# First x tiles loaded one by one between the value rows, in natural token order, and turned by whole 128x128 transposes

## The chip, the cores and the metric

The kernel runs on one core of a Trainium2 chip. The core has five engines with queues of their own, which work at the same time and wait for one another by semaphores: TensorE (PE in the profile, its weight loads PEld), VectorE (DVE), ScalarE (ACT), GpSimd (POOL) and SyncE (SP), which here issues most of the transfers (DMAs). Matmul results land in PSUM, eight banks of 512 float32 columns in 128 partitions; everything else lies in SBUF.

The metric is the device time of one execution in microseconds (us). Before the change it is 283.16 us, the median of three runs (283.02 to 283.38).

## What is computed

A gated mix of two branches over the same x, 2048 tokens of 640 values in bf16: linear attention with 32 heads of 20, and a GELU-gated feed-forward of width 1728.

```python
def _A_ref(x, wqkv, w_phi, wo):
    qkv = (x @ wqkv).reshape(B, S, 3, H, Dh).transpose(2, 0, 3, 1, 4)
    q, k, v = qkv[0], qkv[1], qkv[2]
    pq = einsum("bhsd,hdf->bhsf", q, w_phi)
    pk = einsum("bhsd,hdf->bhsf", k, w_phi)
    phi_q = concatenate([softmax(pq), softmax(-pq)], -1)
    phi_k = concatenate([softmax(pk), softmax(-pk)], -1)
    kv = einsum("bhsf,bhsd->bhfd", phi_k, v)
    z  = einsum("bhsf->bhf", phi_k)
    num = einsum("bhqf,bhfd->bhqd", phi_q, kv)
    den = einsum("bhqf,bhf->bhq", phi_q, z)[..., None] + 1e-6
    return (num / den).transpose(0, 2, 1, 3).reshape(B, S, D) @ wo

def _B_ref(x, w_gate, w_up, w_down):
    return (gelu(x @ w_gate) * (x @ w_up)) @ w_down

g = sigmoid((x * gate_w).sum(-1, keepdims=True))
return g * _A_ref(x, ...) + (1 - g) * _B_ref(x, ...)
```

## The kernel before

**Tiling.** Tokens go in 16 tiles of 128 (`t` = 0 to 15), the 640 model columns in five slices of 128 (`kt`). `xT` holds x turned, 640 rows in five slices by 2048 tokens, because a matmul contracts over the partitions. `w3` holds the value columns of wqkv, one gate column and the folded key and query weights side by side.

**Order.** It is written out by hand: each engine runs its instructions in the order of the program, and a small class (`_Sched`) puts in the semaphore waits from what each operation reads and writes. A PE instruction that waits holds all behind it; so does a waiting copy on DVE or ACT.

**The start.** SP issues, in this order (lines 247 to 262): two loads of the first 512 tokens into `xtok`; the value columns of wqkv, row slice by row slice, the first slice in two pieces (columns 0 to 255 and the rest); a part of w_up (`wue`); the turning transfers of x tiles 4 and 5, of the key weights (`wkT`), of x tiles 6 and 7; another part of w_up (`wul`); the turning transfers of the query weights (`wqT`) and of x tiles 8 to 15. Tiles 0 to 3 are turned on PE instead. In them the tokens are taken with a stride: partition p of tile j holds token 4p + j, so that one load of two tiles reads 2,560 contiguous bytes for a partition, and the output rows of these tiles are written back in the same order (line 919).

ACT issues two small loads, w_phi (line 276, behind the second of POOL's masks) and the gate vector `gz` (line 279).

PE begins in `attention_state` (line 670) with matmuls on constants that nothing reads (line 675). Then come the transposes of tiles 0 and 1 (line 342, 64x64 blocks, ten a tile), six more matmuls on constants (line 682), tiles 2 and 3; each tile goes to PSUM and is copied to `xT` by DVE, by ACT, or by both. Then the value products of tiles 0 to 3 (`v_step`, line 478): for each `kt` and tile a matmul of 480 and one of 160 columns, those of `kt` = 0 cut at column 256. Before the last round `blockdiag` (DVE, line 361) spreads w_phi into block-diagonal tiles, and `gate_column` (line 367) turns the gate vector into a column of `w3`. The finished values are copied out (`v_first_evac`).

**Behind it.** `up_ahead` (line 546) computes three blocks of the feed-forward early, from `wue` and x tiles 0 to 3; then the value tiles 4 and 5, the fold of w_phi into the key weights (`fold`, line 404, reads `wkT` and the block-diagonal tiles), value tiles 6 and 7, key tile 0, two more early blocks from `wul`, the fold into the query weights, and so on through all tiles. The feed-forward and the output follow. The gate's logit of a token tile comes out of one added column, either in the value product or, where `k_gate` (line 560) says so, in the key product.

Of the kernel before, what the change touches and what calls it, by code (L numbers as in the profile page):

```python
# [3 lines left out]
P = 128  # L4
BF16 = mybir.dt.bfloat16
F32 = mybir.dt.float32
AF = mybir.ActivationFunctionType
# [100 lines left out]
class _Kernel:  # L108
    S, D, H, DH, F = 2048, 640, 32, 20, 1728
# [112 lines left out]
    def loads(self):  # L222
# [4 lines left out]
        x4 = self.x[0:self.BT, :].rearrange("(p j) n -> p j n", j=self.TB)  # L227

        def xload(q, j):
            sc.dma(q, lambda e: e.dma_start(self.xtok[:, j:j + 2, :], x4[:, j:j + 2, :]),  # L230
                   writes=[("xtok", j), ("xtok", j + 1)])
# [33 lines left out]
        for i in range(KD):  # L265
# [67 lines left out]
    def x_transpose(self, t, ek):  # L333

        sc = self.sc
        b, w = (0, 4, 2, 6)[t], self.D // 2
        bks = (b, b + 1)
        pv = self.bank(b, 1024).bitcast(BF16).rearrange("p (r c) -> p r c", r=2)[:, :, 0:w]
        for c in range(self.KD):
            for r in (0, 1):  # L340
                a = 64 * r
                sc.op("pe", lambda e: e.transpose(
                    pv[:, r, c * 64:(c + 1) * 64], self.xtok[a:a + 64, t, c * P:(c + 1) * P],
                    self.ident[a:a + 64, a:a + 64]),
                    reads=[("xtok", t), "ident"], writes=[("ps", bks[r])], signal=(c == self.KD - 1))
        out = self.xT[:, :, t * P:(t + 1) * P].rearrange("p c (r t) -> p c r t", t=64)
        src = pv.rearrange("p r (c t) -> p c r t", t=64)
        rd = [("ps", b) for b in bks]
        if ek == "ad":
            sc.op("act", lambda e: e.activation(out[:, :, 0, :], src[:, :, 0, :], AF.Copy), reads=rd[:1], writes=[("xh", t)])  # L350
            sc.op("dve", lambda e: e.tensor_copy(out[:, :, 1, :], src[:, :, 1, :]), reads=rd[1:], writes=[("xT", t)])
        elif ek == "a":
            sc.op("act", lambda e: e.activation(out, src, AF.Copy), reads=rd, writes=[("xT", t)])
        else:
            sc.op("dve", lambda e: e.tensor_copy(out, src), reads=rd, writes=[("xT", t)])
# [117 lines left out]
    def v_step(self, t, kt, part=None):  # L473
        sc = self.sc
        tail = (480, 160, 4 + t // 3, 160 * (t % 3))
        parts = ([(0, self.VA, t, 0)], [(self.VA, 480 - self.VA, t, self.VA), tail], [(0, 480, t, 0), tail])
        for c0, n, bk, col in parts[2 if part is None else part]:
            sc.op("pe", lambda e, c0=c0, n=n, bk=bk, col=col: e.matmul(  # L478
                self.bank(bk)[:, col:col + n], self.xT[:, kt, t * P:(t + 1) * P], self.w3[:, kt, c0:c0 + n],
                start=(kt == 0 and col == 0), stop=(kt == self.KD - 1), skip_group_check=True),  # L480
                reads=[("xT", t), ("xh", t), "wv0" if part == 1 else ("wv", kt)], writes=[("ps", bk)],
                signal=(kt == self.KD - 1))
# [18 lines left out]
    def v_part(self, t, b, part):  # L501
# [4 lines left out]
        self.proj(t, n, self.D + 1 - n, b + 1, 0, ["wv", "wgate"])  # L506
# [4 lines left out]
        self.gate_exp(t, b + 1, o + self.D)  # L511
# [48 lines left out]
    def k_gate(self, t):  # L560
        return 1 if t < self.TB or t == 5 else 0
# [108 lines left out]
    def attention_state(self):  # L670
# [3 lines left out]
        for n in (512, 512, 512, 512, 512, 512, 128, 128, 128):  # L674
# [3 lines left out]
        xt(0, "d")  # L678
        xt(1, "a")
        for i in range(3):  # L680
            for a, b in ((0, 2), (64, 3)):
                sc.op("pe", lambda e: e.matmul(self.bank(b, P), ones[a:a + 64, 0:P], ones[a:a + 64, 0:P], start=True,
                                               stop=True), writes=[("ps", b)])
# [14 lines left out]
        ve([3], "d", True)  # L698
        v, k, q = self.v_tile, self.k_tile, self.q_tile
# [3 lines left out]
        v(4, 2)  # L703
        self.v_split(5, 0)
# [172 lines left out]
    def down_pair(self, t0, banks, widths):  # L877
# [25 lines left out]
        def evac(h):  # L903
# [14 lines left out]
            if t0 < self.TB:  # L918
# [120 lines left out]
```

## Time and profile before

| what | value |
|---|---|
| median of the runs | 283.16 us (283.02 to 283.38) |
| span of the profiled execution | 282.4 us |
| PE busy | 278.6 us, 2926 matmuls |
| DVE busy | 173.2 us |
| ACT busy | 105.9 us |
| POOL busy | 15.1 us |
| granted TensorE clock | 1.000 |
| read from device memory | 9.04 MB |
| written to it | 2.62 MB |

The span runs from the first to the last instruction on the device; the time of a run is a little longer. Times in the timeline count from the span's start. A row of it is a start, a duration, the engine and line, the operation, and what it writes from what it reads; "xN" says that N such instructions in a row are merged. A matmul's duration includes its way through the array, so the spacing of successive starts, not the duration, tells what one costs PE. Transfers are told by the size of each and the time from issue to landing.

The slices of the busy row show where PE is not fully busy: the first of 40 slices (7 us each) has 7 tenths, the last 6 tenths, all others 9 or more.

```profile
PE   7999999999999999999999999999999999999996
...
PEclk9999999999999999999999999999999999999999
DMA  7999169787789910011000000000133132532221
```

### The profile page before, as it was taken

Reading aid. Unit: us, or ns where it says so; the run is one execution under the profiler, and the core shown is the slowest. Engines: PE = TensorE matmul, PEld = TensorE weight load, DVE = VectorE, ACT = ScalarE, POOL = GpSimd, SP = SyncE. Lnnn points to the kernel's source line nnn. Section 1 sums busy time; section 2 is a strip of 40 time slices with the busy share of each in tenths; the row PEclk is TensorE's granted clock in tenths of the full one; section 3 lists DMA queues with packets and bytes.
Section 4 is the critical chain, followed back from the end, with each engine's and each line's share of the span. In section 5 each row is a group of like instructions: output and inputs, shape, how many; then the busy total and the mean of one; then the engine's idle time right before and its main releaser. Section 6 shows DMA issues by size and latency. Waiting matters only on the chain.

```text
span 282.4 us, 6904 instructions
## 1 busy us (share of the span) xinstructions
PE 278.6 (99%) x2926; PEld 168.6 (60%) x2926; DVE 173.2 (61%) x329; ACT 105.9 (38%) x204; POOL 15.1 (5%) x69
## 2 busy tenths in 40 slices
PE   7999999999999999999999999999999999999996
PEld 4566766665665444444444444445777777777786
DVE  1456999999997523694333324235883883883801
ACT  3246978777793332223232232321112112112011
POOL 7511001101000000000000000000000000000000
PEclk9999999999999999999999999999999999999999
DMA  7999169787789910011000000000133132532221
GB/s 213 193 223 190 29 127 172 153 175 149 157 175 274 350 51 0 2 24 23 2 0 0 0 2 0 0 0 2 26 50 98 46 49 78 66 49 73 73 72 49
DMA packets 60378, 24.11 MB, mean 85 GB/s; under 512 B 51002, under 2 KB 59834, under 8 KB 60346
## 3 DMA queue, kind: packets, MB, share of 16 engines
q1 hardware_dynamic: 59680, 23.63, 38.9%
q8 instruction: 23, 0.38, 0.6%
q10 hardware_dynamic: 666, 0.03, 0.2%
q14 instruction: 9, 0.07, 0.1%
HBM read 9.04 MB, written 2.62 MB: 41 GB/s over the span
## 4 chain that ended last, share of the span: by engine, by line
PE 97%; DMA 1%; SPq 0%; ACT 0%; issue 0%
PE ps L464 58%; PE ps L898 29%; PE ps L599 4%; PE ps L817 2%; PE ps L478 2%; PE ps L637 2%; DMA w<-in_A_wqkv_dram 1%; PE ps L404 1%; SPq L230 0%; SPq L251 0%; ACT outsb L911 0%; PE ps L370 0%
## 5 line engine op out<-in xcount | busy, mean ns | idle before, releaser
L464 PE MATMUL ps<-xT,wu_sb 128*128 128x512 bf16 x260 | 64.1, 379 | 0.0
L464 PE MATMUL ps<-xT,wg_sb 128*128 128x512 bf16 x260 | 63.9, 379 | 0.0
L779 ACT ACTIVATE gl<-ps 128x512 bf16<-128x512 f32 x52 | 31.0, 597 | 70.3 <-PE ps L464 70.3
L464 PE MATMUL ps<-w,xT 128*128 128x362 bf16 (+5 forms) x340 | 51.4, 302 | 0.0
L898 PE MATMUL ps<-wd_sb,hT 64*128 64x320 bf16 x648 | 48.4, 296 | 0.0
L781 DVE TENSOR_TENSOR hT<-ps,gl 128x512 bf16<-128x512 f32 x34 | 23.4, 689 | 37.7 <-PE ps L464 37.7
L464 PEld LDWEIGHTS ps<-xT,wu_sb 128*128 128x128 bf16 x260 | 25.4, 98 | 30.3 <-DVE hT L781 0.2
L464 PEld LDWEIGHTS ps<-xT,wg_sb 128*128 128x128 bf16 x260 | 25.1, 98 | 29.8 <-issue 0.2
L911 ACT ACTIVATE outsb<-ps,Gm 128x320 bf16<-128x320 f32 (+2 forms) x31 | 14.5, 515 | 71.8 <-PE ps L898 71.8
L464 PEld LDWEIGHTS ps<-w,xT 128*128 128x128 bf16 x340 | 31.9, 97 | 14.8
L898 PEld LDWEIGHTS ps<-wd_sb,hT 64*128 64x128 bf16 x648 | 30.9, 94 | 12.2 <-issue 0.4
L898 PE MATMUL ps<-wo_sb,goT 64*128 64x320 bf16 (+2 forms) x340 | 26.5, 288 | 0.0
L617 DVE TENSOR_REDUCE Dk<-Ek 128x66 f32<-128x1320 bf16 x16 | 24.3, 1520 | 2.3 <-ACT gcol L528 2.3
L626 DVE TENSOR_TENSOR Ek<-Ek,Dk 128x1320 bf16<-128x1320 bf16 x16 | 24.5, 1532 | 0.5
L863 DVE TENSOR_TENSOR O<-ps,RH 128x640 bf16<-128x640 f32 x32 | 24.7, 815 | 0.0
L538 ACT ACTIVATE Ek<-ps 128x627 bf16<-128x627 f32 x32 | 20.5, 693 | 6.4 <-PE ps L599 4.9
L538 ACT ACTIVATE Eqt<-ps 128x627 bf16<-128x627 f32 x32 | 20.6, 705 | 2.5 <-PE ps L464 2.5
L781 DVE TENSOR_TENSOR xT<-ps,gl 128x512 bf16<-128x512 f32 x13 | 9.0, 690 | 18.2 <-PE ps L464 18.2
L898 PEld LDWEIGHTS ps<-wo_sb,goT 64*128 64x128 bf16 x340 | 15.9, 94 | 5.3
L898 PE MATMUL ps<-wd_sb,xT 64*128 64x320 bf16 (+2 forms) x270 | 16.0, 269 | 0.0
L851 DVE RECIPROCAL RH<-ps 128x32 f32<-128x32 f32 x16 | 5.7, 357 | 14.4 <-PE ps L817 14.3
L898 PEld LDWEIGHTS ps<-wd_sb,xT 64*128 64x128 bf16 x270 | 12.1, 94 | 2.7
(90 smaller groups left out, 184.1 us busy)
## 6 DMA issues: line engine op xcount, KB each, us to landing
out_dram<-outsb SPq DMA_DIRECT2D x7, 320.0 KB, 2.3
wd_sb<-in_B_w_down_dram SPq DMA_DIRECT2D x1, 2080.0 KB, 11.0
wg_sb<-in_B_w_gate_dram SPq DMA_DIRECT2D x5, 224.0 KB, 3.1
wg_sb<-in_B_w_gate_dram SPq DMA_DIRECT2D x5, 192.0 KB, 3.5
wu_sb<-in_B_w_up_dram SPq DMA_DIRECT2D x5, 192.0 KB, 3.9
wo_sb<-in_A_wo_dram SPq DMA_DIRECT2D x1, 800.0 KB, 9.7
xtok<-in_A_x_dram SPq DMA_DIRECT2D x2, 320.0 KB, 3.3
w<-in_A_wqkv_dram SPq DMA_DIRECT2D x4, 160.0 KB, 4.0
```

Source lines behind the costliest of these rows:

```text
L464: self.sc.op("pe", lambda e: e.matmul(self.ps[:, bank * 512 + c0:bank * 512 + c0 + n], lhs, rhs, start=first, stop=fin), reads=reads, writ ...
L478: sc.op("pe", lambda e, c0=c0, n=n, bk=bk, col=col: e.matmul(self.bank(bk)[:, col:col + n], self.xT[:, kt, t * P:(t + 1) * P], self.w3[:, ...
L538: self.sc.op("act", lambda e: e.activation(dst, src, AF.Exp, scale=scale), reads=[("ps", b), ("ps", b + 1)], writes=[(name, sl, s)])
L599: self.sc.op("pe", lambda e: e.matmul(out, self.xT[:, kt, t * P:(t + 1) * P], self.w3[:, kt, c:c + 2 * n].rearrange("p (r w) -> p r w", w= ...
L617: self.sc.op("dve", lambda e: e.tensor_reduce(self.Dk[:, se, 0, :].rearrange("p (u h) -> p u h", h=self.HG), self.k_view(se), AX.X, ALU.ad ...
L626: sc.op("dve", lambda e: e.tensor_tensor(v, v, R.rearrange("p (u h) -> p u h", h=self.HG).unsqueeze(3).to_broadcast([P, 2 * self.G, self.H ...
L779: sc.op("act", lambda e: e.activation(self.gl[:, slot, :], self.bank(banks[0]), AF.Gelu_apprx_tanh), reads=[("ps", banks[0])], writes=[("g ...
L781: sc.op("dve", lambda e: e.tensor_tensor(hT, up, self.gl[:, slot, :], ALU.mult), reads=[upk, ("gl", slot)], writes=[("hT", hk, c)], guard=old)
L851: dve(lambda e: e.reciprocal(R(0), Dn[1]), rb, [key(0)], guard=old)
L863: dve(lambda e, o=o, f=f, s=s: e.tensor_tensor(o, V[s][:, :, 0:DH], f, ALU.mult), rb + [key(6 + s)], [("O", s, sl)], guard=old)
L898: sc.op("pe", lambda e: e.matmul(self.bank(bk, w), lhs, rhs, start=opens and x == 0, stop=end and not opens, skip_group_check=True), reads ...
L911: sc.op("act", lambda e: e.activation(dst, self.bank(bk, w), AF.Copy, scale=g), reads=rd, writes=wr)
```

## The change

- x tiles 0 to 3 are loaded in natural token order, one load for each tile (160 KB), and these loads alternate with the value row slices: x0, w0, x1, w1, x2, w2, x3, w3, w4. The first value slice comes in one piece.
- A tile is turned by five whole 128x128 transposes. The first three slices go to one PSUM bank and are copied by DVE (key `xh`), the last two to the next bank and are copied by ACT (key `xT`). Value steps with `kt` < 3 wait for the first copy only.
- PE starts with four matmuls of 512 columns and four of 128 on constants instead of six and three; the six small ones behind the first tile have 128 rows instead of 64. The value steps are interleaved with the transposes of the next tiles.
- The loads of w_phi and of the gate vector are issued from ACT behind the last x copy. `blockdiag` moves behind the copies of the first values.
- `gate_column` moves behind value tile 4. The gate logit of tile 4 moves from its value product to its key product.
- The output rows of tiles 0 to 3 are written in natural order.

```diff
-        x4 = self.x[0:self.BT, :].rearrange("(p j) n -> p j n", j=self.TB)
+        x4 = self.x[0:self.BT, :].rearrange("(j p) n -> p j n", p=P)
 
         def xload(q, j):
-            sc.dma(q, lambda e: e.dma_start(self.xtok[:, j:j + 2, :], x4[:, j:j + 2, :]),
-                   writes=[("xtok", j), ("xtok", j + 1)])
+            sc.dma(q, lambda e: e.dma_start(self.xtok[:, j, :], x4[:, j, :]), writes=[("xtok", j)])
...
-        xload("sp", 0)
-        xload("sp", 2)
         for kt in range(KD):
-            for a, z, key in ((0, self.VA, ("wv", 0)), (self.VA, D, "wv0")) if kt == 0 else ((0, D, ("wv", kt)),):
-                sc.dma("sp", lambda e: e.dma_start(self.w3[:, kt, a:z], w3[:, kt, 2 * D + a:2 * D + z]), writes=[key])
+            if kt < self.TB:
+                xload("sp", kt)
+            sc.dma("sp", lambda e: e.dma_start(self.w3[:, kt, 0:D], w3[:, kt, 2 * D:3 * D]), writes=[("wv", kt)])
...
-        sc.dma("act", lambda e: e.dma_start(
-            self.wphi_sb[:, :, :], self.wphi.rearrange("h d f -> (h d) f").rearrange("(i p) f -> p i f", p=P)),
-            reads=[("mask", 1)], writes=["wphi"])
-        sc.dma("act", lambda e: e.dma_start(self.gz[0:KD, :], self.gw.rearrange("(k p) -> k p", p=P)), writes=["gz"])
...
+    def x_transpose(self, t):
 
         sc = self.sc
+        b = (6, 2, 6, 6)[t]
+        for ek, bk, c0, c1, key in (("dve", b, 0, 3, "xh"), ("act", b + 1, 3, 5, "xT")):
+            pv = self.bank(bk).bitcast(BF16)[:, 0:(c1 - c0) * P].rearrange("p (c t) -> p c t", t=P)
+            for c in range(c0, c1):
+                sc.op("pe", lambda e: e.transpose(pv[:, c - c0, :], self.xtok[:, t, c * P:(c + 1) * P], self.ident[:, :]),
+                      reads=[("xtok", t), "ident"], writes=[("ps", bk)], signal=c == c1 - 1)
+            out = self.xT[:, c0:c1, t * P:(t + 1) * P]
+            sc.op(ek, lambda e: e.tensor_copy(out, pv) if ek == "dve" else e.activation(out, pv, AF.Copy),
+                  reads=[("ps", bk)], writes=[(key, t)])
...
+    def v_step(self, t, kt):
+        for c0, n, bk, col in ((0, 480, t, 0), (480, 160, 4 + t // 3, 160 * (t % 3))):
+            self.sc.op("pe", lambda e: e.matmul(
...
+                reads=[("xh" if kt < 3 else "xT", t), ("wv", kt)], writes=[("ps", bk)], signal=(kt == self.KD - 1))
...
-        self.proj(t, n, self.D + 1 - n, b + 1, 0, ["wv", "wgate"])
+        g = 1 - self.k_gate(t)
+        self.proj(t, n, self.D + g - n, b + 1, 0, ["wv"] + ["wgate"] * g)
...
     def k_gate(self, t):
-        return 1 if t < self.TB or t == 5 else 0
+        return 1 if t <= self.TB + 1 else 0
...
-        for n in (512, 512, 512, 512, 512, 512, 128, 128, 128):
+        for n in (512, 512, 512, 512, 128, 128, 128, 128):
...
-        xt(0, "d")
-        xt(1, "a")
-        for i in range(3):
-            for a, b in ((0, 2), (64, 3)):
-                sc.op("pe", lambda e: e.matmul(self.bank(b, P), ones[a:a + 64, 0:P], ones[a:a + 64, 0:P], start=True,
-                                               stop=True), writes=[("ps", b)])
-        xt(2, "d")
-        xt(3, "ad")
-        for t, part in ((0, 0), (1, 0), (0, 1), (1, 1), (2, 0), (2, 1), (3, 0), (3, 1)):
-            vs(t, 0, part)
-        for kt in range(1, 4):
-            for t in range(4):
-                vs(t, kt)
-        self.blockdiag()
-        self.gate_column(6)
+        xt(0)
+        for i in range(6):
+            sc.op("pe", lambda e: e.matmul(self.bank(0, P), ones[:, 0:P], ones[:, 0:P], start=True, stop=True),
+                  writes=[("ps", 0)])
+        vs(0, 0)
+        xt(1)
+        for t, kt in ((0, 1), (1, 0), (1, 1)):
+            vs(t, kt)
+        xt(2)
+        for t, kt in ((0, 2), (1, 2)):
+            vs(t, kt)
+        xt(3)
+        self.small_loads()
+        for t, kt in ((2, 0), (2, 1), (2, 2), (0, 3), (1, 3), (2, 3), (3, 0), (3, 1), (3, 2), (3, 3)):
+            vs(t, kt)
         for t in range(4):
             vs(t, 4)
             ve([t], "ad"[t % 2], False)
...
         ve([3], "d", True)
+        self.blockdiag()
...
         v(4, 2)
+        self.gate_column(6)
```

`small_loads` holds the two ACT loads that were taken out of `loads`, without the wait for the mask.

More of the change, by code (lines that the diff above doesn't have):

```diff
@@ L331, in down_weights @@
         self.load(self.wo_sb[:, :, :], self.wo.rearrange("(kt p) n -> p kt n", p=P), "wo")
-    def x_transpose(self, t, ek):
+    def x_transpose(self, t):
         sc = self.sc
[L336 to L355, printed above, removed]
@@ L357, in blockdiag, with small_loads @@
+    def small_loads(self):
+        sc = self.sc
+        sc.dma("act", lambda e: e.dma_start(
+            self.wphi_sb[:, :, :], self.wphi.rearrange("h d f -> (h d) f").rearrange("(i p) f -> p i f", p=P)),
+            writes=["wphi"])
+        sc.dma("act", lambda e: e.dma_start(self.gz[0:self.KD, :], self.gw.rearrange("(k p) -> k p", p=P)), writes=["gz"])
     def blockdiag(self):
@@ L510, in v_part @@
             reads=[("ps", b), ("ps", b + 1), ("vone", sv)], writes=[("vaug", sv)])
-        self.gate_exp(t, b + 1, o + self.D)
+        if g:
+            self.gate_exp(t, b + 1, o + self.D)
     def v_split(self, t, b):
@@ L917, in evac @@
                 return
-            if t0 < self.TB:
-                rows = self.out[0:self.BT, :].rearrange("(p j) n -> p j n", j=self.TB)[:, t0:t0 + 2, :]
-            else:
-                rows = self.out[t0 * P:(t0 + 2) * P, :].rearrange("(j p) n -> p j n", p=P)
+            rows = self.out[t0 * P:(t0 + 2) * P, :].rearrange("(j p) n -> p j n", p=P)
             sc.dma("sp", lambda e: e.dma_start(rows[:, :, c0:c1], self.outsb[:, os_:os_ + 2, c0:c1]),
```

8 lines of the change are left out of this document (removed).

## The prediction

> **What bounds the kernel now.** I read the page's busy times and its chain first, then TensorE's (PE's) timeline from the start, then SP's issues with their landings, last the copies between them.
>
> ```profile
> span 282.4 us, 6904 instructions
> PE 278.6 (99%) x2926; PEld 168.6 (60%) x2926; DVE 173.2 (61%) x329; ACT 105.9 (38%) x204; POOL 15.1 (5%) x69
> ...
> PE 97%; DMA 1%; SPq 0%; ACT 0%; issue 0%
> ```
>
> PE is busy all the time and the chain is 97% PE. The waits of PE in the whole trace are 0.8 us at launch and 0.4 us for a value row (wqkv). Only the first 11.5 us hold time that isn't needed:
>
> ```profile
> 0.84 3.04 PE L675 MATMUL ps<-const-bfloat16-1.0 128*128 128x512 bf16 x9 [0.84 <-PEq L1024]
> 3.99 0.47 PE L342 MATMUL ps<-ident,xtok 64*128 64x64 bf16 x20
> 4.29 0.34 PE L682 MATMUL ps<-const-bfloat16-1.0 64*128 64x128 bf16 x6
> 4.77 0.47 PE L342 MATMUL ps<-ident,xtok 64*128 64x64 bf16 x20
> 5.37 0.38 PE L478 MATMUL ps<-w,xT 128*128 128x256 bf16 x2
> 6.19 4.35 PE L478 MATMUL ps<-w,xT 128*128 128x224 bf16 x34 [0.44 <-DMA w<-in_A_wqkv_dram]
> 10.38 0.22 PE L370 MATMUL ps<-ident,gz 128*128 128x128 bf16 x1
> 10.44 1.25 PE L478 MATMUL ps<-w,xT 128*128 128x480 bf16 x8
> 11.53 3.40 PE L464 MATMUL ps<-xT,wu_sb 128*128 128x512 bf16 x15
> ```
>
> Columns: start, duration. Fillers on constants run until x arrives at 3.99; the transposes and two short products are scattered up to 5.37; the value products run unbroken only from 6.19. `up_ahead` starts at 11.53, and PE waits for no transfer after it. So the start of `up_ahead` is the marker: what it moves, the end moves.
>
> What set those times are the landings (issue times from SP's timeline, 0.47 us apart from 0.80 on):
>
> ```profile
> xtok<-in_A_x_dram SPq DMA_DIRECT2D x1, 320.0 KB, 3.1
> ...
> w<-in_A_wqkv_dram SPq DMA_DIRECT2D x1, 64.0 KB, 3.5
> ...
> w<-in_A_wqkv_dram SPq DMA_DIRECT2D x1, 96.0 KB, 3.9
> ...
> wu_sb<-in_B_w_up_dram SPq DMA_DIRECT2D x5, 64.0 KB, 2.4
> wphi_sb<-in_A_w_phi_dram ACTq DMA_DIRECT2D x1, 25.0 KB, 4.5
> ```
>
> The last column is us from issue to landing. x: 0.80+3.1 = 3.9. First value piece: 1.73+3.5 = 5.2; second: 2.20+3.9 = 6.1, which is the 6.19.
>
> **The change, part by part.**
>
> *Loads.* Two x loads of 320 KB and a first value row in two pieces become x0, w0, x1, w1, x2, w2, x3, w3, w4, 160 KB each, issued at 0.80 + 0.47 k. No row has a 160 KB load with an empty queue ahead. Bounds: 3.1 (320 KB, above) and 2.4 (64 KB). In proportion to size 2.4+0.7*96/256 = 2.66; I take 2.7. The queues aren't overrun: 160 KB per 0.467 us is 351 GB/s, and the half-microsecond stretches of before reach 405. Landings: x0 3.50, w0 3.97, x1 4.43, w1 4.90, x2 5.37, w2 5.83, x3 6.30, w3 6.77, w4 7.23.
>
> *Transposes.* 40 of 64x64 become 20 of 128x128. Before: 20 in 0.47-0.19 = 0.28 us (0.19 is one's latency in the tile's view), so 0.14 a tile. After: the gate transpose of the same shape takes 10.44-10.38 = 0.056 of PE, five are 0.28 a tile, 0.56 more for four tiles; the first tile stands before the products either way, and between them they cost 0.28 each.
>
> *Copies.* Each tile is copied in two halves that run side by side, DVE 384 columns and ACT 256:
>
> ```profile
> 4.45 0.49 DVE L355 COPY xT<-ps 128x640 bf16<-128x640 bf16 x1 [4.45 <-PE ps L342]
> ...
> 5.64 0.32 DVE L351 COPY xT<-ps 128x320 bf16<-128x320 bf16 x1
> ```
>
> DVE: 0.32+0.17*64/320 = 0.35. ACT's rows are 0.70 (640) and 0.44 (320), so 0.39. A value step needs only DVE's half while kt < 3.
>
> *The new start, step by step.* A value step (480+160 columns) is (11.53-10.44)/4 = 0.273. x0 3.50 -> transposes at 3.55 (before 3.94 -> 3.99); three done 3.85; DVE copy to 4.21; with 0.1 for the handover (before, pieces landed at 5.24 and 6.15 and their products began at 5.37 and 6.19) v(0,0) 4.31-4.58 (the six fillers of 128 columns, 0.34, end by 4.17). Transposes of x1 to 4.86; w1 4.90 -> v(0,1) 4.95-5.22; x1's DVE half ends 4.88+0.35 = 5.24 -> v(1,0) and v(1,1) 5.34-5.88; x2 to 6.16; v(0,2), v(1,2) to 6.71; x3 to 6.99; fourteen steps of 0.273 to 10.81. `up_ahead` starts 11.53-10.81 = **0.72 us earlier**. The fewer fillers (they end at 2.97) cost nothing: they end before x0.
>
> *Gate column.* The transpose moves behind v(4) and costs 0.056 at either place. Its DVE copy is needed by v(6) only. Tile 4's column moves from v(4) to k(4): 5 columns each, zero sum.
>
> *w_phi and gate_w.* They leave the ACT queue at about 7.6 behind the last x copy (their issues, 0.43 and 0.67, lie in ACT's idle 5.1 us before its first value copy). w_phi lands 7.6+4.5 = 12.1. DVE now waits there for it, with `up_ahead`'s copies, the gate copy and v_split's copy queued behind. `blockdiag` (1.18) then ends at 13.3 and the two `up_ahead` copies (0.69 each) by 14.9. The fold reads these at 17.59-0.72 = 16.87, so w_phi may land as late as 16.87-1.18-1.38 = 14.3 at no cost. Later than that each us is one.
>
> *Transfers behind.* One more issue on SP pushes all behind it by 0.47. Least slack: x tiles 6, 7 land 13.69+3.9 = 17.6 and are read at 18.75 (1.1); wkT 8.86+7.5 = 16.4 against 17.59 (1.2); `wue` 4.57+5.7 = 10.3 against 11.53 (1.2). Upper bound of the push: 0.47 plus the ACT queue's 666 small packets (w_phi above all), which now fall among these. Before, they stood at 4.0 to 5.5 us, where throughput was 219, 251 and 215 GB/s against about 335 behind: some 160 KB, 0.48 us. Lower bound: these packets no longer delay what goes ahead, -0.48. I take 0, as SP stands 3.77 us in the issue of x tiles 4, 5 and only 1.40 us in that of 6, 7 of the same size: by that it waits for room, which now comes no later.
>
> *Output.* Tiles 0 to 3 are written in natural order like all others, off the path. Nothing.
>
> **Sum.** The profiled execution has 282.4 us, the median is 283.16, so 0.7 lies around it. 283.16-0.72 = **282.44**. Landing bounds: at 2.4 all is 0.3 earlier, 282.14; at 3.1 0.4 later, 282.84.
>
> **Rivals.**
>
> *The clock rises late (slower).* The fillers of 512 columns start 0.43 us apart:
>
> ```profile
> 1.22 0.63 PE L675 MATMUL ps<-const-bfloat16-1.0 128*128 128x512 bf16 x1
> 1.65 0.63 PE L675 MATMUL ps<-const-bfloat16-1.0 128*128 128x512 bf16 x1
> ```
>
> and the `up_ahead` matmuls of the same width 0.215 (15 in 3.40). So PE runs at half speed at first, though the granted clock shows 1.00 throughout; by 4.3 the fillers of 128 columns are 0.057 apart, full speed. Before, PE had been busy from 0.84 to 3.67. Now it stops at 2.97 and stands about 0.6 us. If the rise comes from that early work and is missed, PE stays slow. Priced with a rise that takes as long again as it did (0.84 to 3.99, 3.15 us), at 7.1: x0's transposes and fillers 3.55-4.75, v(0,0) to 5.30, x1 5.83, v(0,1), v(1,0) 6.90, v(1,1) 7.32, x2, two steps, x3 8.43, fourteen steps 12.25, 0.72 later than before: 283.88. It decides once the rise is later than about 5 us (0.72 gained is 1.44 us at half speed). For it: two fillers of six are gone. Against: the rise came within 3.2 us of the first filler, across a gap. The Trainium skill (TensorE: Matmul & The Clock Gate, Part 1, "What's actually happening") says that activity over a free-running window of about 3.4 us lifts the half rate, and its Part 4 that transposes do not count as busy; by that a window with less work in it may fail and the next be needed. The trace agrees with the half rate; where its windows lie no row shows.
>
> *The late transfers cap it.* With the full push of 0.95, tiles 6 and 7 leave 1.1-0.95 = 0.2 of gain: 282.96. For it: DVE's and SP's queues are in order and the DMA share is about 1 at 5 to 9 us. Against: the full slack now, and fewer bytes stuck early.
>
> *The 160 KB pieces take what the value rows took (3.9).* Then w0 5.17, x1 5.63, w1 6.10: v(0,0) 5.22, x1 to 5.96, v(0,1) 6.42, v(1,0) and v(1,1) to 6.98, x2, two steps to 7.81, x3 8.09, `up_ahead` at 11.9, 0.38 late: 283.54. Against: these rows had 640 KB of x and w_phi ahead of them.
>
> **How the numbers follow.** Forecast 58%, clock 27%, capped 8%, late pieces 7%. A measurement tells about 0.2%, 0.57 us, from no change. The forecast's own range is 282.14 to 282.84, of which some four fifths are beyond 0.57: faster 0.46. Its rest, the capped case and most of the late pieces: same 0.25. The clock and a little of the late pieces: slower 0.29. The range must reach the clock case: 282.1 to 283.95.
>
> **What would show it.** Right: x0's transposes at about 3.5, the first value step at 4.3, no PE wait over 0.1 after 5, `up_ahead` at 10.8, chain still PE. Wrong: v steps 0.53 apart at 5 us (clock); a PE wait for xT or wkT at 16 to 18 (cap); waits for w rows at 5 to 7 (late pieces); DVE waiting for w_phi beyond 14.3.

## The result, and the profile after

The changed kernel takes 284.95 us (284.76 to 285.98), the kernel before beside it 283.18: a ratio of 1.0062, interval 1.0041 to 1.0083. It is slower by 1.77 us where 0.72 us less was forecast. A later repeat, ten runs, gave a smaller loss: 284.18 against 283.26, ratio 1.0035 (1.0022 to 1.0047). I take the repeat's +0.92 us as the size; where the first measurement's larger value comes from is said below.

The page of the changed kernel:

```profile
span 284.7 us, 6842 instructions
PE 279.2 (98%) x2887; PEld 169.8 (60%) x2901; DVE 173.2 (61%) x330; ACT 106.4 (37%) x206; POOL 15.2 (5%) x69
...
PE 96%; DMA 2%; SPq 1%; issue 0%; ACT 0%
```

PE still sets the end, but the chain now has 2% DMA. PE's timeline of the start (start, duration, as before):

```profile
0.84 2.29 PE L663 MATMUL ps<-const-bfloat16-1.0 128*128 128x512 bf16 x8 [0.84 <-PEq L1011]
3.09 0.71 PE L334 MATMUL ps<-ident,xtok 128*128 128x128 bf16 x5
3.60 0.85 PE L668 MATMUL ps<-const-bfloat16-1.0 128*128 128x128 bf16 x6
4.39 0.69 PE L465 MATMUL ps<-w,xT 128*128 128x480 bf16 x2
4.88 0.74 PE L334 MATMUL ps<-ident,xtok 128*128 128x128 bf16 x5
5.41 1.59 PE L465 MATMUL ps<-w,xT 128*128 128x480 bf16 x6
6.91 0.45 PE L334 MATMUL ps<-ident,xtok 128*128 128x128 bf16 x5
7.58 0.72 PE L465 MATMUL ps<-w,xT 128*128 128x480 bf16 x4 [0.23 <-DMA w<-in_A_wqkv_dram]
8.14 0.44 PE L334 MATMUL ps<-ident,xtok 128*128 128x128 bf16 x5
8.42 4.00 PE L465 MATMUL ps<-w,xT 128*128 128x480 bf16 x28
12.47 0.38 PE L454 MATMUL ps<-xT,wu_sb 128*128 128x512 bf16 x1
```

L334 are the transposes of one tile, L465 the value steps. Five transposes take 0.71 to 0.74 at first and 0.44 later, three value steps 1.59 at first, two of them 0.72 later: half speed until about 6.6. The third tile is turned only at 6.91, the fourth at 8.14. (The record of the first `up_ahead` matmul is missing here and in some profiles below; it began 0.215 earlier, at 12.26. Where it is missing, marker times below are so corrected.) The landings, from the DMA views of single issues (the last column is us from issue to landing); first x0, then x2, w2 and x3:

```profile
xtok<-in_A_x_dram SPq DMA_DIRECT2D x1, 160.0 KB, 2.2
...
xtok<-in_A_x_dram SPq DMA_DIRECT2D x1, 160.0 KB, 4.2
...
w<-in_A_wqkv_dram SPq DMA_DIRECT2D x1, 160.0 KB, 4.4
...
xtok<-in_A_x_dram SPq DMA_DIRECT2D x1, 160.0 KB, 4.4
```

So x0 came sooner than the 2.7 us of the forecast, everything from x2 on far later. The windows of one us show it as throughput (last column, GB/s; the one ahead of it is the DMA share). Before:

```profile
4.00:5.00 1.00, 0.85 (x42) 0.68 (x44) 0.49 (x1) 0.41 (x1) 0.72 (x6) 1.00 0.92 235
5.00:6.00 1.00, 0.62 (x20) 0.24 (x10) 0.72 (x2) 0.71 (x2) 0.78 (x8) 1.00 1.06 270
6.00:7.00 1.00, 0.81 (x9) 0.79 (x10) 0.00 (x0) 0.00 (x0) 1.00 (x10) 1.00 1.08 332
```

After:

```profile
4.00:5.00 1.00, 1.00 (x9) 0.56 (x7) 0.00 (x0) 0.23 (x1) 0.72 (x6) 1.00 1.05 339
5.00:6.00 1.00, 1.00 (x9) 0.71 (x8) 0.36 (x1) 0.35 (x1) 0.78 (x7) 1.00 0.58 126
6.00:7.00 1.00, 1.00 (x8) 0.47 (x6) 0.00 (x0) 0.03 (x1) 1.00 (x10) 1.00 0.85 205
```

Between 5 and 7 us, when x2, w2 and x3 should land, about half as many bytes move as before (in the repeat 245 and 187 GB/s).

Little is lost or won behind the marker: from it to the last matmul's end are 268.77 us before (280.30-11.53) and 268.85 after (281.11-12.26); the gate column's transpose, 0.056, now lies behind it. The other part of this execution's span lies at its very end: the last output lands 3.58 us after the last matmul instead of 2.09. The repeat had 2.1 again. The first measurement's median is larger for another reason: it lies between the runs of 284.89 and 285.01, whose spans of 282.7 and 283.0 are like the repeat's (median 282.8), but which have 2.2 and 2.0 us outside the span where most runs have 1.2 to 1.3.

The steps beside the forecast (us; "repeat" is the changed kernel again, "fillers" the changed kernel with the first fillers of before):

| start of | forecast | first | repeat | fillers |
|---|---|---|---|---|
| x0's transposes | 3.55 | 3.09 | 3.14 | 3.67 |
| v(0,0) | 4.31 | 4.39 | 4.29 | 4.65 |
| x1's transposes | 4.58 | 4.88 | 4.82 | 5.02 |
| v(0,1) | 4.95 | 5.41 | 5.36 | 5.48 |
| x2's transposes | 5.88 | 6.91 | 6.36 | 6.37 |
| v(0,2) | 6.16 | 7.58 | 6.81 | 6.65 |
| x3's transposes | 6.71 | 8.14 | 7.61 | 7.67 |
| `up_ahead` | 10.81 | 12.26 | 11.74 | 11.80 |
| (x3 landed) | 6.30 | 8.02 | 7.57 | 7.62 |

### The profile page after: what moved, and what is told of

Read it like the earlier page. It is cut to its first block, busy times and chain, and to the rows that moved or that the text cites. A ratio compares the mean times of both kernels' runs of the same rounds, so it can differ in the third digit from the quotient of the medians.

```text
span 284.7 us, 6842 instructions
## 1 busy us (share of the span) xinstructions
PE 279.2 (98%) x2887; PEld 169.8 (60%) x2901; DVE 173.2 (61%) x330; ACT 106.4 (37%) x206; POOL 15.2 (5%) x69
## 4 chain that ended last, share of the span: by engine, by line
PE 96%; DMA 2%; SPq 1%; issue 0%; ACT 0%
PE ps L454 57%; PE ps L888 28%; PE ps L587 4%; PE ps L807 2%; PE ps L625 2%; PE ps L465 2%; DMA w<-in_A_wqkv_dram 2%; PE ps L394 1%; SPq L230 0%; SPq L249 0%; ACT outsb L901 0%; PE ps L334 0%; PE ps L360 0%
## 5 line engine op out<-in xcount | busy, mean ns | idle before, releaser
L454 PE MATMUL ps<-xT,wu_sb 128*128 128x512 bf16 x256 | 63.2, 379 | 0.3
L454 PE MATMUL ps<-xT,wg_sb 128*128 128x512 bf16 x250 | 61.8, 379 | 0.5 <-issue 0.2
L454 PE MATMUL ps<-w,xT 128*128 128x362 bf16 (+6 forms) x340 | 51.5, 302 | 0.0
```

The source lines that it names most:

```text
L454: self.sc.op("pe", lambda e: e.matmul(self.ps[:, bank * 512 + c0:bank * 512 + c0 + n], lhs, rhs, start=first, stop=fin), reads=reads, writ ...
```

## The experiments

Times are medians; the ratio is to the kernel before, run beside them on the same chip (its medians there were 283.26 to 283.50). Two theories stood against each other from the start: the clock (fewer fillers), and the late landings of the alternating loads.

**a_again: the changed kernel once more.** No edit.

> The changed kernel once more, unaltered, to see what repeats. Its profile had PE at half speed until 6.5 us (transposes 0.107 apart), x2 landing 4.2 us after its issue (6.9 us) and the last output transfer taking 3.1 us instead of 1.6. Clock theory: half speed until about 6.5 again, early feed-forward blocks start at about 12.5, time about 1.8 us over the kernel before. Transfer theory: x2 again lands near 6.9 us. If the last output transfer lands in 1.6 us here while the time stays 1.8 over, that transfer is not part of the cause.

284.18, ratio 1.0035 (1.0022 to 1.0047). Its timeline:

```profile
4.82 0.74 PE L334 MATMUL ps<-ident,xtok 128*128 128x128 bf16 x5
5.36 1.17 PE L465 MATMUL ps<-w,xT 128*128 128x480 bf16 x6
6.36 0.44 PE L334 MATMUL ps<-ident,xtok 128*128 128x128 bf16 x5
6.81 0.72 PE L465 MATMUL ps<-w,xT 128*128 128x480 bf16 x4
7.61 0.45 PE L334 MATMUL ps<-ident,xtok 128*128 128x128 bf16 x5
7.90 4.00 PE L465 MATMUL ps<-w,xT 128*128 128x480 bf16 x28
```

Half speed ends inside the six matmuls at 5.36, at about 5.7. The delay against the forecast is 0.48 by 6.36, 0.65 by 6.81 (w2 landed at 6.77), 0.90 by 7.61 (x3 landed at 7.57).

**a_fill: the changed kernel with the first fillers of before.**

```diff
-        for n in (512, 512, 512, 512, 128, 128, 128, 128):
+        for n in (512, 512, 512, 512, 512, 512, 128, 128, 128):
```

> The changed kernel with the kernel before's opening fillers (six of 512 and three of 128 columns instead of four and four). Clock theory: full speed by 4.0 us, x0's transposes start at 3.7 instead of 3.1 but the value steps run 0.27 apart; if the transfers land early enough the early blocks start at about 11.3 and the time falls by about 1.2 us against the changed kernel. Transfer theory: full speed too, but PE waits for x2 (6.9) and w2 (7.5), the early blocks start at 12.4 and the time stays within 0.2 us of the changed kernel.

284.12, ratio 1.0032 (1.0016 to 1.0047): no gain.

```profile
5.02 0.45 PE L334 MATMUL ps<-ident,xtok 128*128 128x128 bf16 x5
5.48 1.06 PE L465 MATMUL ps<-w,xT 128*128 128x480 bf16 x6
6.37 0.44 PE L334 MATMUL ps<-ident,xtok 128*128 128x128 bf16 x5
6.65 0.71 PE L465 MATMUL ps<-w,xT 128*128 128x480 bf16 x4
7.67 0.45 PE L334 MATMUL ps<-ident,xtok 128*128 128x128 bf16 x5 [0.31 <-DMA xtok<-in_A_x_dram]
```

Full speed from about 4.4 on, but x1 landed at 4.97, and the time won is waited away at x3 (0.31). The marker, 11.80, is no earlier than the repeat's 11.74.

**b_fewfill: the kernel before with the fewer fillers.** The same line the other way round.

> The kernel before with the changed kernel's opening fillers (four of 512, four of 128 columns). Clock theory: half speed until about 6.5 to 7 us, the first transposes and value steps cost double, early blocks start 0.3 to 1.0 us later than 11.53, time 0.3 to 1.0 us over the kernel before. If the number of fillers does not matter: early blocks at 11.5, time within 0.2 us of the kernel before.

284.20 (282.98 to 285.04), ratio 1.0025 (1.0009 to 1.0042). In the profiled execution the transposes began at 3.91, on time, and then:

```profile
5.42 6.36 PE L478 MATMUL ps<-w,xT 128*128 128x256 bf16 x36
...
11.68 1.26 PE L478 MATMUL ps<-w,xT 128*128 128x480 bf16 x8
12.99 0.38 PE L464 MATMUL ps<-xT,wu_sb 128*128 128x512 bf16 x1
```

The 36 matmuls start 0.77 sooner than the unbroken run of before and take 6.36: half speed to 9.1, marker 12.77. In the kernel before, the fewer fillers thus cost time by themselves, and the cost varies: the shortest run is level with the best of before, the longest 2 us above.

**b_natural: the kernel before with natural token order only** (x loads of two tiles with 1,280 contiguous bytes instead of 2,560, output rows to match).

```diff
-        x4 = self.x[0:self.BT, :].rearrange("(p j) n -> p j n", j=self.TB)
+        x4 = self.x[0:self.BT, :].rearrange("(j p) n -> p j n", p=P)
```

> The kernel before with the natural token order alone (two x loads of 320 KB in runs of 1,280 bytes instead of 2,560, output rows of tiles 0 to 3 in natural order). Transfer theory in the form that the natural order slows the x loads: x lands 0.3 to 0.8 us later, early blocks start at 11.8 to 12.3, time 0.3 to 0.8 us over. If the order does not matter: x lands at 3.9 and 4.7, time within 0.2 us of the kernel before.

283.61, ratio 1.0020 (0.9997 to 1.0042), no difference shown: eight of the ten runs lie at 283.24 to 283.74, two at 285.7 and 285.8, and what sets these two apart was not profiled. In the profiled execution the two x loads landed at 3.73 and 4.80, marker 11.22. There the order cost nothing.

**b_swap: the kernel before, second x load behind the whole first value row**, steps of tiles 0 and 1 first.

```diff
-        xload("sp", 0)
-        xload("sp", 2)
         for kt in range(KD):
+            if kt < 2:
+                xload("sp", 2 * kt)
```

> A try at a version that beats both: the kernel before (64x64 transposes, strided pair loads, its fillers) with the second x pair loaded behind the first value row, that row in one piece, step (0,0) taken before tiles 2 and 3 are turned, and the steps of tiles 0 and 1 for the slices 0 to 2 before those of tiles 2 and 3. First value step at 5.0 and no wait behind it: early blocks at 10.75 to 10.9, time 0.3 to 0.5 us under the kernel before. If w2 lands late as in the changed kernel (6.6): a wait at (0,2), early blocks at 11.1, no gain. If the transfers behind become the limit (0.3 us of slack left): PE waits for wkT or x tiles 6 and 7 at 16 to 18 us, no gain.

284.47, ratio 1.0048 (1.0027 to 1.0070). The second load landed at 5.99, 4.3 us after its issue (3.5 before); PE waited 0.59 for it and 0.17 for a row; marker 12.05. An x load behind a row comes late also with 320 KB pieces, full fillers and, in this execution, full speed from 4.1 on.

**a_oldorder: the changed kernel with the loads and the step order of before** (x in two natural loads ahead of the rows, all transposes first) and its fillers; whole transposes, halved copies, late small loads and gate column stay.

```diff
-            if kt < self.TB:
-                xload("sp", kt)
...
+        for j in (0, 2):
+            sc.dma("sp", lambda e: e.dma_start(self.xtok[:, j:j + 2, :], x4[:, j:j + 2, :]),
+                   writes=[("xtok", j), ("xtok", j + 1)])
...
+        xt(2)
+        xt(3)
+        self.small_loads()
+        for kt in range(4):
+            for t in range(4):
+                vs(t, kt)
```

> The changed kernel with three things put back as they were: the loads (two x loads of two tiles each, here in natural order, ahead of the five value rows), the order of PE's work (all four x tiles turned first, then the value steps slice by slice over the four tiles) and the opening fillers. Kept of the change: whole 128x128 transposes, split copies, natural order, late w_phi and gate column. Theory that the alternating loads and the order that hangs on them cost the time: back to the kernel before within 0.3 us (its value stage ends at about 11.1 to 11.5). Theory that the whole transposes (0.56 us more) or the late small loads cost it: 0.5 us or more over the kernel before.

284.49, ratio 1.0038 (1.0023 to 1.0053).

```profile
3.74 1.25 PE L335 MATMUL ps<-ident,xtok 128*128 128x128 bf16 x10
...
5.43 1.11 PE L335 MATMUL ps<-ident,xtok 128*128 128x128 bf16 x10
6.38 5.64 PE L466 MATMUL ps<-w,xT 128*128 128x480 bf16 x40
```

The second x load landed at 5.38, and only then could the other ten transposes run, ahead of every value step: marker 11.86. Half speed lasted to 6.2 here, with nine fillers. This pointed at the whole transposes as a third cost.

**b_whole: the kernel before with whole transposes and halved copies only** (`x_transpose` of the changed kernel; every value step still waits for both halves).

> The kernel before, with one change: each of the first x tiles is turned by five whole 128x128 transposes and copied by DVE (384 columns) and ACT (256). Loads, order, fillers and w_phi stay. Theory A (the whole transposes are the larger part of the loss, as they stand at half speed between x and the value steps, 1.1 us for two tiles in place of 0.5): value steps unbroken only from about 6.4, marker about 11.6 to 11.9, 0.4 to 0.8 us slower. Theory B (the alternating loads are the loss, and the transposes are covered by the wait for the first value row): unbroken from 6.2 at the latest, marker 11.2 to 11.5, within 0.2 us of before.

284.41 (283.35 to 284.99), ratio 1.0034 (1.0021 to 1.0046), but the profile doesn't put the loss where theory A has it:

```profile
3.90 1.24 PE L340 MATMUL ps<-ident,xtok 128*128 128x128 bf16 x10
...
5.35 0.73 PE L340 MATMUL ps<-ident,xtok 128*128 128x128 bf16 x10
5.92 4.56 PE L467 MATMUL ps<-w,xT 128*128 128x256 bf16 x36
```

The first ten transposes ran at half speed, the next at full speed, and the value steps were unbroken from 5.92, sooner than the 6.19 of before; marker 11.46, last matmul's end 280.23 against 280.30. In this execution the transposes were covered. Its span was longer at the end (last output 2.9 us behind the last matmul), and in five of eleven runs 1.9 to 2.2 us lie outside the span, where before has 1.25. So the ratio is not explained by the transposes, and what it is due to stays open.

**a_64_fill: the changed kernel with full fillers and 64x64 transposes.**

```diff
-                sc.op("pe", lambda e: e.transpose(pv[:, c - c0, :], self.xtok[:, t, c * P:(c + 1) * P], self.ident[:, :]),
+            for r in (0, 1):
+                a = 64 * r
+                sc.op("pe", lambda e: e.transpose(pv[:, r, c * 64:(c + 1) * 64], self.xtok[a:a + 64, t, c * P:(c + 1) * P], self.ident[a:a + 64, a:a + 64]),
```

> The changed kernel with the fillers of before and with the 64x64 transposes of before; each tile is copied by DVE (one half of its tokens) and ACT (the other), and every value step waits for both. Theory A (transposes): with 0.14 to 0.25 us a tile in place of 0.28 to 0.55, the marker moves ahead by 0.4 us or more of that of the changed kernel with fillers (11.80), and the time falls by as much, to about 283.7. Theory B (the rows and x3 land too late): PE waits longer for w2 and x3 instead, the marker stays at 11.7 to 11.8 and the time at about 284.1.

284.35, ratio 1.0034 (1.0022 to 1.0046), marker 11.84. Transposes 0.14 a tile cheaper bring nothing here; PE waited 0.27 for ACT's half of x1's copy instead (whole steps now need both halves). Theory A is not borne out for the changed kernel, though this version has a wait of its own.

**a_wphi_early, b_wphi_late: the place of w_phi.** The first issues w_phi and the gate vector at the old place in the changed kernel, the second issues w_phi behind the last x copy in the kernel before (`blockdiag` behind the value copies).

> The changed kernel with the w_phi and gate loads back at their early place. Theory that the 640 small packets take transfer time from the x and value rows: these land 0.3 to 0.5 us later from x1 or w1 on, early blocks 0.3 to 0.5 us later, time 284.5 to 284.7. If the rows are slow for another reason (the changed kernel's throughput falls to 180 to 200 GB/s at 5.5 to 7 us with no small packet near): no change, 284.2.

> The kernel before with the w_phi load alone moved behind its last x copy, and blockdiag behind the first value copies. Theory that the small packets slow the rows: second value piece at 5.7 instead of 6.1, early blocks at 10.8 to 11.3, time 0.2 to 0.5 us under the kernel before (282.8 to 283.0). If they do not matter: same within 0.15 us. If the waiting blockdiag blocked DVE: a PE wait at 13 to 18 us and a slower kernel.

284.27, ratio 1.0030 (1.0014 to 1.0045), and 283.51, ratio 0.9995 (0.9985 to 1.0005). The place of w_phi costs and brings nothing that shows. In the first, x2 landed at 5.96 and x3 at 7.76, later than in the repeat (5.70 and 7.57) and sooner than in the first profile (6.86 and 8.02): the small packets are not what slows the rows.

These two profiles also say something of the clock. In a_wphi_early, with eight fillers, full speed came at 4.0, and PE waited for x1 (0.29) and x3 (0.40) instead; the marker was 11.93, later than the repeat's:

```profile
4.16 0.43 PE L469 MATMUL ps<-w,xT 128*128 128x480 bf16 x2
4.88 0.45 PE L338 MATMUL ps<-ident,xtok 128*128 128x128 bf16 x5 [0.29 <-DMA xtok<-in_A_x_dram]
...
7.81 0.45 PE L338 MATMUL ps<-ident,xtok 128*128 128x128 bf16 x5 [0.40 <-DMA xtok<-in_A_x_dram]
...
11.93 1.02 PE L458 MATMUL ps<-xT,wu_sb 128*128 128x512 bf16 x4
```

In b_wphi_late, with nine fillers, the transposes ran at half speed (0.71 where before has 0.47), which lasted to 6.4; the marker was 11.40:

```profile
4.73 0.71 PE L339 MATMUL ps<-ident,xtok 64*128 64x64 bf16 x20
```

**a_x3late, a_x3late_fill, a_x3mid: x3 turned later**, so that its landing can't be waited for; the second with full fillers, the third between v(2,2) and v(0,3).

```diff
-        xt(3)
-        self.small_loads()
-        for t, kt in ((2, 0), (2, 1), (2, 2), (0, 3), (1, 3), (2, 3), (3, 0), (3, 1), (3, 2), (3, 3)):
+        for t, kt in ((2, 0), (2, 1), (2, 2), (0, 3), (1, 3), (2, 3)):
             vs(t, kt)
+        xt(3)
+        self.small_loads()
+        for t, kt in ((3, 0), (3, 1), (3, 2), (3, 3)):
+            vs(t, kt)
```

> The changed kernel with the turning of x tile 3 (and the small loads behind it) moved behind the six value steps (2,0), (2,1), (2,2), (0,3), (1,3), (2,3), which do not need it. In the changed kernel's repeat x3 landed at 7.57 us, PE had stood 0.24 us for it, and the fourteen steps behind it run unbroken to the early blocks at 11.96. Theory that the landing of x3, seventh of nine loads, sets the end of the value stage: early blocks 0.2 to 0.5 us earlier (11.5 to 11.75), time 0.2 to 0.5 us under the changed kernel. Clock theory (half speed costs, the transfers do not): no change, 284.2.

> The same with the opening fillers of the kernel before as well. If clock and landing each hide the other, this is the first version of the change in which the clock shows: another 0.2 to 0.5 us under a_x3late, early blocks at 11.2 to 11.5. If w2 (landing about 6.7) is then what PE waits for, the fillers change nothing: the same as a_x3late within 0.15 us.

> The changed kernel with x3's turning between (2,2) and (0,3), so that neither its landing nor its copy is waited for (in a_x3late the wait for the landing became a 0.49 us wait for the copy). Landing theory in this form, that what comes behind w2's landing (6.6 to 6.8 us) is fixed at sixteen steps of 0.273 and one turning of 0.28, 4.65 us: early blocks at 11.3 to 11.45, 0.3 us under the changed kernel's repeat (11.74), time about 283.9. If PE still waits elsewhere: 11.7 or later, 284.2.

284.56 (1.0036; 1.0024 to 1.0047), 284.54 (1.0047; 1.0030 to 1.0064), 284.10 (1.0026; 1.0016 to 1.0036). In a_x3late the wait for the landing is gone and another is in its place:

```profile
8.97 0.44 PE L334 MATMUL ps<-ident,xtok 128*128 128x128 bf16 x5
9.76 2.36 PE L465 MATMUL ps<-w,xT 128*128 128x480 bf16 x16 [0.34 <-DVE xT L337]
```

With no step left to cover it, x3's own copy stands on the path; markers 11.96, and 11.99 with full fillers. In a_x3mid it is covered, but x2 landed at 6.73 and PE waited 0.59 for it; marker 11.87. Its time is +0.77 over before, where the repeat has +0.92; the intervals don't tell the two apart.

**a_hold, a_hold_turn_fill, a_64_hold_fill: the transfers behind the rows held back.** In the first (one run), SP waits for w4 before it issues `wue` and all behind it; in the second, with full fillers, for w3 before the turning transfers; the third adds the 64x64 transposes.

```diff
-        sc.dma("sp", lambda e: e.dma_start(self.wu_sb[:, :, a:z], u3[:, :, a:z]), writes=["wue"])
+        sc.dma("sp", lambda e: e.dma_start(self.wu_sb[:, :, a:z], u3[:, :, a:z]), reads=[("wv", 4)], writes=["wue"])
```

> The changed kernel with one wait added: SP issues everything behind the value rows (w_up part, turned x tiles, key weights) only when the last value row has landed. It will be slower by 2 to 4 us and is only looked at for the landings. Theory that issuing the turning transfers at 5.5 us slows the rows in flight: no dip of throughput at 5.5 to 7 us (300 GB/s and more), x3 lands by 6.5, w3 by 7.0. If the rows are slow by themselves (runs of 1,280 bytes): x3 at 7.2 to 7.6 and w3 at 7.8 to 8.1 as in all other versions.

> The changed kernel with the fillers of before, and SP waits for value row 3 before it issues the turning transfers; the w_up piece is issued ahead of them as before. Theory B (the turning transfers in flight at 5 to 7 us slow the rows and x3): x3 lands by 7.1 and w3 by 7.5, marker 11.3 to 11.5, 0.3 to 0.5 us less than the changed kernel with fillers, about 283.7, if x tiles 6 and 7 and the key weights still land by 18 us; if they do not, PE waits for them at 17 to 19 us. Theory A (transposes): the marker stays at 11.7 to 11.8 and the time at 284.1.

> Both edits on the changed kernel with the fillers of before: 64x64 transposes and the turning transfers held behind value row 3. If each of the two parts is real and they are in series, the marker comes to 10.9 to 11.2 and the time to 283.0 to 283.3, level with before or a little ahead; if one of them hides the other, it stays with the better of the two single ones.

284.22; 284.18 (1.0034; 1.0022 to 1.0047); 284.50 (1.0037; 1.0024 to 1.0050). In a_hold:

```profile
7.54 4.00 PE L465 MATMUL ps<-w,xT 128*128 128x480 bf16 x28
12.19 0.59 PE L454 MATMUL ps<-xT,wu_sb 128*128 128x512 bf16 x2 [0.65 <-DMA wu_sb<-in_B_w_up_dram]
```

x3 landed at 7.08 instead of 7.57, w4 at 7.99 instead of 9.39. This is one execution, and with nothing held x3 came at 7.15 in a_x3late and w4 at 8.52 in a_x3mid: the transfers behind seem to slow the last row, for x3 it isn't shown. And `wue` then comes too late and takes 0.65 back. With only the turning transfers held, x3 landed at 7.40 and w2 at 6.63; half speed lasted to 5.9 in that execution, and the marker stayed at 11.90. The parts don't add up: the third is no better (marker 12.16).

**b_2q, a_2q_fill: part of x issued from ACT**, ahead of its first activation: the second load of before; x1 and x3 of the changed kernel, with full fillers.

```diff
-        xload("sp", 2)
+        xload("act", 2)
```

```diff
-            if kt < self.TB:
+            if kt in (0, 2):
                 xload("sp", kt)
...
+        xload("act", 1)
+        xload("act", 3)
```

> The kernel before, with the second load of x (tiles 2 and 3, 320 KB) issued from ACT ahead of its first activation instead of from SP; everything behind it on SP is issued 0.47 us earlier. If what counts is the time of issue: w0's two pieces land 0.47 us earlier (4.8 and 5.7), value steps unbroken from 5.8, marker 11.1 instead of 11.53, about 0.4 us faster (0.9985). If the bytes in flight set the landings (1.28 MB landed by 8.0 us whatever the order): second piece of w0 still at 6.1, marker 11.4 to 11.6, within 0.2 us of before.

> The changed kernel with the fillers of before and x tiles 1 and 3 issued from ACT at the start; SP issues x0, w0, w1, x2, w2, w3, w4. All of x is then under way 1.9 us sooner for x1 and x3 (issue about 0.8 and 1.3). If the time of issue counts: x1 lands by 3.9 and x3 by 4.5, w rows 0.5 to 0.9 us earlier than in the changed kernel with fillers, no PE wait for x3, marker 10.9 to 11.2, time 283.0 to 283.4. If the bytes in flight set the landings: x1 and x3 early, but w0 to w2 later by as much; PE waits for the rows, marker 11.5 to 11.8, time 283.8 to 284.1.

283.69 (1.0025; 1.0008 to 1.0041) and 284.90 (1.0051; 1.0031 to 1.0070). In a_2q_fill x1 and x3 landed at 3.63 and 4.83, but x0 at 3.84 instead of 3.12 (a_fill), w0 at 5.03 instead of 3.55, and w2 at 6.52 as in a_fill (6.55): marker 11.77. Pieces that are issued sooner push the others back; the bytes in flight set the landings, not the issuing queue. In b_2q the two x loads were under way together and both landed after 4.5 (the first had 3.94). PE stood for 0.91, and in the profiled execution the rise of the clock was missed:

```profile
4.79 0.71 PE L342 MATMUL ps<-ident,xtok 64*128 64x64 bf16 x20 [0.91 <-DMA xtok<-in_A_x_dram]
...
6.29 5.82 PE L478 MATMUL ps<-w,xT 128*128 128x256 bf16 x36
```

Half speed to 8.9, marker 13.09. Its twelve times form two groups: eight of 283.40 to 283.76 and four of 285.00 to 285.38. The profiled execution (span 284.0) is of the upper group; that the other three missed the rise as well is inferred.

## Why the prediction was wrong

**What held.** The marker: what moves `up_ahead` moves the last matmul, to 0.1 us in every profile. At full speed the durations: five transposes 0.27 to 0.29, DVE's half 0.36, ACT's 0.38, a step 0.273. w_phi landed at 12.7 (8.63+4.1), `blockdiag` ran at 13.2 and cost nothing; and PE waited for no turned tile or key weight at 16 to 18 us, so the capped case did not occur.

**Where it failed: "The queues aren't overrun ... Landings: x0 3.50, ... x3 6.30".** One latency of 2.7 us was given to nine pieces. It grew along the row: in the repeat 2.3, 2.3, 2.9, 2.9, 3.0, 3.6, 3.9, 3.9, 4.8 us. By 8.0 us 1,280 KB of x and value rows had landed in the profile of before and in the repeat alike, whatever the order (1,120 KB by 8.02 in the first profile; 1,440 KB at most, in a_hold and a_2q_fill among others). The evidence stood in the same trace: throughputs of 215 to 251 GB/s at 4.0 to 5.5 us, which the working put down to w_phi's packets (with w_phi moved away, b_wphi_late still fell to 196 GB/s at 4.5 to 5.0), and 3.9 us for a row, which it put down to the x ahead of it. The size of the piece was taken for what sets its landing; with equal sizes it went by the place in the row. The Trainium skill (DMA: Bandwidth & Descriptors, "Latency and other measured facts") says that memory latency rises from 0.2 us on average to 2 us at high load. The growth here, 2.5 us from issue to landing, is of that size, but no row tells memory latency from waiting behind other pieces.

**What that decides.** Before, all of x is there at 4.73, and each row of 160 KB opens four steps, 1.09 us of work, so only the first row can be late: the marker of that profile is w0's landing (6.15) plus 5.38. After, the seventh of nine pieces, x3, has 4.17 us of work behind it (11.74-7.57 in the repeat; 4.18 and 4.17 in a_fill and a_wphi_early, where PE had full speed from 4.4 and 4.0 on; 4.24 at first, 12.26-8.02). To win against the profiled execution of before, x3 had to land before 11.53-4.17 = 7.36; it was forecast for 6.30 and came at 7.57 to 8.02 in these four.

**Second failure: "The fewer fillers ... cost nothing: they end before x0".** PE was at half speed until 6.6 in the first profile and 5.7 in the repeat, so transposes and steps before that took about twice the time of the forecast. The rival had 27% and named this mechanism; its rise at 7.1 was later than either, so that its marker of 12.25 is the first profile's 12.26 is luck (there x3's landing at 8.02 set it). But the changed kernel does not need half speed to lose: in a_fill and a_wphi_early full speed came at 4.4 and 4.0, and x2's transposes still began at 6.37 and 6.24 (repeat 6.36, forecast 5.88), because w1 landed at 5.43 and 5.34 instead of 4.90. And the number of fillers did not alone decide when the rise came (see the last section). What the fewer fillers cost is shown for the kernel before (b_fewfill, 1.0025); for the changed kernel no run shows a cost. The case of late pieces, 7%, gave a marker of 11.9 (11.74 measured in the repeat) with a uniform 3.9. The two cases were treated as alternatives; in the first two profiles they stood side by side and hid one another: full fillers don't help while x3 lands late, and an x3 that isn't waited for leaves its own copy (a_x3late) or x2's landing (a_x3mid). So neither can be given a share of the 0.92 us alone.

**The base of the sum.** The gain of 0.72 was counted from one execution and taken off the median of others. In most runs 1.2 to 1.3 us lie outside the span, not 0.7, and the median span of before is 282.0 to 282.3, so the profiled execution, 282.4, was longer than usual. Its w0 was late: the second piece landed at 6.15, but at 5.26 to 5.64 in b_fewfill, b_natural, b_whole and b_wphi_late, which issue x and the rows in the same order. Two of these, with spans of 282.1 and 282.3, have markers of 11.22 and 11.40. So part of the 0.72 seems to be the chance of that one execution, and against a usual one x3 had to land even sooner than 7.36. The sum also counts the gate transpose, 0.056, as won at the marker, though it only moves behind it.

**Open.** That the late landings make up the whole 0.92 us is not shown: they explain the marker of the profiled executions, but b_whole and a_oldorder, which have the load order of before, lose as much (1.0034 and 1.0038). What they share with the changed kernel are the whole transposes with their halved copies, and with these goes a longer end of the run. In 16 of the 99 runs of kernels that have them, 1.8 to 2.6 us lie outside the span; in none of the 62 runs of the versions without them, nor of 120 runs of before (1.2 to 1.4). Why, no run shows, and b_whole's loss is not all of this kind: its median span is 282.7 where before has 282.1. Nor is it shown why throughput falls to 126 to 205 GB/s at 5 to 7 us in the first profile; w_phi has no part in it. No version beat the kernel before; b_wphi_late is level with it.

## What to carry to other kernels

When loads are reordered to start sooner, take each landing from a transfer at the same place in the row of bytes, not of the same size, and ask how much work hangs behind the last piece that the new order needs: work that was open to all pieces and is now tied to a late one has lost its slack. Take the base from more than one execution: the one profiled here had a late first row. Before an early stage is made to begin sooner, ask whether PE will be at full speed by then, and look at several executions, for the time of the rise varied by over 2 us. When one repair changes nothing, look for a second cost of about the same size that it uncovers.

## What the runs showed of the hardware

- When full speed came, read from the spacing of starts, varied from execution to execution. With nine first fillers it came between 4.0 (before) and 6.4 us (b_wphi_late) in twelve profiles, and at 8.9 in b_2q, where PE had stood for 0.91. With eight it came between 4.0 (a_wphi_early) and 6.6 (first profile) in six, and at 9.1 in b_fewfill, where PE had stood for 0.79. In a_hold_turn_fill it came at 5.9 although PE had issued without a break from 0.84 on. The granted clock in the windows read 1.00 all the while. The Trainium skill (TensorE: Matmul & The Clock Gate, Part 1, "What's actually happening") gives a free-running window of about 3.4 us as the reason for a variation of 0.5 us either way; the spread here is wider, and no row shows a window. Its Part 4 says that the full rate does not engage for transposes; here it did, 0.056 us apart against 0.107 before the rise (both in the repeat).
- Times fell into two groups in b_2q (four of twelve runs 1.2 us or more above the others), b_swap (four of ten, about 1 us) and b_natural (two of ten, 1.9 us). Only one run of an upper group was profiled, the b_2q run with the rise at 8.9; that the rise parts the groups is inferred.
- The last output landed 2.1 us behind the last matmul in sixteen of twenty profiles, but 2.9 in b_whole, 3.3 in a_hold_turn_fill, 3.6 in the first profile of the changed kernel and 3.8 in a_oldorder, all four with whole transposes; no run says why.
